# A scaled residual sum: the first 30.5 KiB of each partition taken from a contiguous head of the tensors

## The chip, the core and the metric

The kernel runs on one core of one Trainium2 chip. The core has a VectorE (DVE in the profile), a TensorE (PE), a ScalarE, a GpSimd (POOL) and a SyncE (SP), an on-chip memory of 128 partitions, and 16 DMA engines that move data between that memory and DRAM. In this kernel every transfer is issued from one queue, that of SyncE (SPq). The metric is the time of one execution on the device, in microseconds; the median of three runs is given.

## The reference

```python
B, S, D = 512, 32, 640          # x, fx: (B, S, D) bf16; alpha: (1,) bf16

def reference(x, fx, alpha):
    return x + alpha * fx
```

Each of x, fx and the output has 10,485,760 elements, 20.97 MB. The kernel reads 41.94 MB and writes 20.97 MB.

## The kernel before

Every tensor is seen as 128 rows, one for each partition, of 160 KiB each: partition p takes the elements from p x 81,920 on. The program counts in units of K = 512 elements, which are 1 KiB in bf16, so `x 0 64` is the load of the first 64 KiB of each partition's row, 128 rows of 64 KiB that lie 160 KiB apart in DRAM. (A row of over 64 KiB is cut into two equal pieces.)

There is one buffer `t` in the on-chip memory, of 207.5 KiB a partition (ROW = 160 and SPARE = 47.5). A piece of x from a to b is loaded to the places a to b of `t`, is added to in place, and is stored from there. The pieces of fx are put wherever there is space: the third number of an `f` step is its place in `t`. The places 95 to 160, for instance, first hold fx 0 to 65, and only later x 95 to 160; 160 to 207.5 first hold fx 65 to 112.5, and later fx 112.5 to 160. So the load of x from 95 on has to wait until the additions on 0 to 65 have read their fx, and the last two loads of fx wait for the additions on 65 to 95 and on 95 to 112.5.

The order is written out by hand in the string `PLAN`, one step a line, and the program issues the steps in that order, each on its engine:

- `f a b p` (L98 to L100): load fx from a to b to the place p; issued on SPq
- `x a b` (L95, L96): load x from a to b to its own place; SPq
- `a` (L102 to L110): load alpha eight times over, spread it over 128 partitions with a matmul, and copy the result to `a_f`
- `m a b` (L112, L113): multiply fx from a to b by alpha in place; VectorE, TENSOR_SCALAR
- `c a b` (L115, L116): add fx to x from a to b, in place of x; VectorE, TENSOR_TENSOR
- `s a b` (L118, L119): store from a to b; SPq
- `| m 112.5 134.5` behind a store: it also waits until that step has been done

An engine takes its steps strictly in order, and a step waits for the data it needs and for the space it overwrites. After the last store stands a no-operation on SPq (L131) that waits for everything but the last store. The function `of` (L86) says where in a DRAM tensor the piece from a to b of all partitions lies, and `xv`, `fv`, `ov` (L67) are the tensors as 128 rows.

The plan before, with its steps on one line each queue:

```text
SPq:     f 0 8 | a | f 8 65 | x 0 64 | x 64 95 | f 65 112.5 | x 95 160 |
         f 112.5 142.5 | f 142.5 160 | s 0 64 | s 64 128 | s 128 160
VectorE: m 0 8 | m 8 65 | c 0 8 | c 8 64 | c 64 65 | m 65 95 | c 65 95 |
         m 95 112.5 | c 95 112.5 | m 112.5 134.5 | m 134.5 142.5 |
         c 112.5 142.5 | m 142.5 160 | c 142.5 160
```

The first six loads wait for nothing. The first store waits for `m 112.5 134.5`, the second for `c 112.5 142.5`, the third for `c 142.5 160`.

Of the kernel before, what the change touches and what calls it, by code (L numbers as in the profile page):

```python
# [1 line left out]

# [4 lines left out]

ALU = mybir.AluOpType
F32 = mybir.dt.float32

P = 128
K = 512
ROW = 160
SPARE = 47.5

LANES = 8

PLAN = """
f 0 8 95
a
f 8 65 103  # L30
x 0 64
x 64 95
f 65 112.5 160
m 0 8
m 8 65
c 0 8
c 8 64
c 64 65
x 95 160
m 65 95  # L40
c 65 95
f 112.5 142.5 160
m 95 112.5
c 95 112.5
f 142.5 160 190
m 112.5 134.5
s 0 64 | m 112.5 134.5
m 134.5 142.5
c 112.5 142.5
m 142.5 160  # L50
c 142.5 160
s 64 128
s 128 160
"""


@with_exitstack
def kernel(
    ctx: ExitStack,
    tc: tile.TileContext,  # L60
    x: bass.AP,
    fx: bass.AP,
    alpha: bass.AP,
    out: bass.AP,
):
    nc = tc.nc
    xv, fv, ov = (  # L67
        t.flatten_outer_dims().rearrange("(p n) d -> p (n d)", p=P) for t in (x, fx, out)
    )
    assert xv.shape[1] == ROW * K  # L70

    consts = ctx.enter_context(tc.tile_pool(name="consts", bufs=1))
    psum = ctx.enter_context(tc.tile_pool(name="psum", bufs=1, space=bass.MemoryType.PSUM))
    flat = ctx.enter_context(tc.tile_pool(name="flat", bufs=1))
    ctx.enter_context(tc.manual_schedule())
    t = flat.tile([P, int((ROW + SPARE) * K)], x.dtype, name="t")
    info = mybir.DependencyInfo(mybir.DependencyClass.Sync, mybir.DependencyReason.DATA)

    lanes = {}
    lies = []  # L80
    done = []

    def at(a, b):
        return t[:, int(a * K) : int(b * K)]

    def of(v, a, b):  # L86
        return v[:, int(a * K) : int(b * K)]

    def place(a, b):
        for c, d, p in reversed(lies):  # L90
            if c <= a and b <= d:
                return at(p + a - c, p + b - c)
        raise ValueError(f"fx {a} to {b} lies nowhere in one piece")

    def load_x(a, b):  # L95
        done.append(nc.sync.dma_start(out=at(a, b), in_=of(xv, a, b)))  # L96

    def load_f(a, b, p):  # L98
        lies.append((a, b, p))
        done.append(nc.sync.dma_start(out=at(p, p + b - a), in_=of(fv, a, b)))  # L100

    def load_alpha():  # L102
        a_n = consts.tile([LANES, 1], alpha.dtype, name="a_n")
        done.append(nc.sync.dma_start(out=a_n[:], in_=alpha[None, :].to_broadcast([LANES, 1])))  # L104
        ones = consts.tile([1, P], alpha.dtype, name="ones")
        nc.vector.memset(ones[:], 1.0)  # L106
        a_ps = psum.tile([P, 1], F32, name="a_ps")
        done.append(nc.tensor.matmul(a_ps[:], ones[:], a_n[0:1, :], start=True, stop=True))  # L108
        lanes["a"] = consts.tile([P, 1], F32, name="a_f")
        nc.vector.tensor_copy(out=lanes["a"][:], in_=a_ps[:])  # L110

    def multiply(a, b):  # L112
        done.append(nc.vector.tensor_scalar_mul(place(a, b), place(a, b), lanes["a"][:]))  # L113

    def add(a, b):  # L115
        done.append(nc.vector.tensor_add(at(a, b), at(a, b), place(a, b)))  # L116

    def store(a, b):  # L118
        done.append(nc.sync.dma_start(out=of(ov, a, b), in_=at(a, b)))  # L119

    does = {"x": load_x, "f": load_f, "a": load_alpha, "m": multiply, "c": add, "s": store}
    begun = {}
    for step in filter(None, PLAN.split("\n")):
        step, *later = step.split(" | ")
        what, *numbers = step.split()
        does[what](*map(float, numbers))
        begun[step] = done[-1]
        for other in later:
            tc.add_manual_dep(done[-1].ins, begun[other].ins.name, info, reason="begins late")

    rest = nc.sync.nop(nofuse=True)  # L131
    for i in done[:-1]:
        tc.add_manual_dep(rest.ins, i.ins.name, info, reason="all but the last store")


# [1 line left out]
_INS = ['x', 'fx', 'alpha']  # L137
_OUTS = [((512, 32, 640), 'bfloat16')]


# [23 lines left out]
```

## Time and profile before

| | |
|---|---|
| median of 3 runs | 151.1 us (151.07 to 151.1) |
| the profiled execution | 151.11 us |
| its span, from the first to the last instruction | 149.3 us |
| DMA engines: busy share of the span | 98.0% |
| read from DRAM, written to it | 41.94 MB, 20.97 MB |
| mean rate over the span | 421 GB/s |
| VectorE busy | 66.5 us (45%) |
| of it additions (L116), multiplications (L113) | 43.6 us, 22.8 us |

The profiled execution's time, 151.11 us, is 1.8 us longer than its span: what lies before the first and after the last instruction is in the time and not in the span. The busy share of the DMA queue is the time that its packets took, over 16 engines and the span. A packet is one contiguous row or piece of a row, and every DMA adds some of a few bytes for its semaphore. In the slices of the page, and of the close-ups of the DMA, a packet is counted in the slice in which it starts, so long packets make high and low slices in turn while the engines are evenly busy.

Costliest groups by shape, with busy time and the mean of one, from the list of groups kept apart by shape:

| line | operation | elements a partition | count | mean ns |
|---|---|---|---|---|
| L116 | add | 28672 | 1 | 15086 |
| L116 | add | 15360 | 2 | 8157 |
| L116 | add | 8960 | 2 | 4826 |
| L116 | add | 4096 | 1 | 2293 |
| L113 | multiply | 29184 | 1 | 7820 |
| L113 | multiply | 15360 | 1 | 4220 |
| L113 | multiply | 11264 | 1 | 3152 |
| L113 | multiply | 8960 | 2 | 2546 |

### The profile page before, as it was taken

The page shows a single profiled execution, that of the slowest core. Times are in us where ns is not written, and L with a number is a line of the kernel's source. Part 1 is how long each engine was busy: PE and PEld are TensorE (multiplying, and loading weights), DVE is VectorE, ACT ScalarE, POOL GpSimd, SP SyncE. Part 2 cuts the span into 40 slices and gives each one's busy share as a digit, 9 for nine tenths or more (in the row PEclk, how much of TensorE's full clock was granted, in tenths as well). Part 3 has the DMA queues.
Part 4 walks back from the last instruction along what each step waited for, and adds up shares of the span by engine and source line. Part 5 has one row for each costly group of instructions (what it writes and reads, how often), then busy time and mean ns, then how long its engine had stood idle before and what let it go on. Part 6 is the DMA issues. An engine that isn't in the chain of part 4 may idle for free.

```text
span 149.3 us, 84 instructions
## 1 busy us (share of the span) xinstructions
PE 0.2 (0%) x1; PEld 0.1 (0%) x1; DVE 66.5 (45%) x16; POOL 0.2 (0%) x4
## 2 busy tenths in 40 slices
PE   0000000000000000000000000000000000000000
PEld 0000000000000000000000000000000000000000
DVE  0300008920069999029997093599997000000000
POOL 0000000000000000000000000000000000000000
DMA  5969998969699999999999999899896969697993
GB/s 147 603 281 500 500 461 351 562 281 562 281 408 451 438 417 443 456 429 428 428 428 428 417 444 469 378 526 492 351 562 281 562 281 562 281 562 307 456 474 167
DMA packets 1728, 62.92 MB, mean 421 GB/s; under 512 B 192, under 2 KB 192, under 8 KB 192
## 3 DMA queue, kind: packets, MB, share of 16 engines
q1 hardware_dynamic: 1728, 62.92, 98.0%
HBM read 41.94 MB, written 20.97 MB: 421 GB/s over the span
## 4 chain that ended last, share of the span: by engine, by line
DMA 38%; DVE 33%; another core or an unknown queue 4%; SPq 1%; issue 0%; DVEq 0%
DMA t<-in_x_dram 27%; DVE t L116 26%; DMA t<-in_fx_dram 11%; DVE t L113 7%; SPq L100 0%; SPq L104 0%; DVEq L116 0%
## 5 line engine op out<-in xcount | busy, mean ns | idle before, releaser
L116 DVE TENSOR_TENSOR t<-t 128x15360 bf16<-128x15360 bf16 (+4 forms) x7 | 43.6, 6252 | 16.6 <-DMA t<-in_x_dram 16.5
L113 DVE TENSOR_SCALAR t<-t,a_f 128x4096 bf16<-128x4096 bf16 (+4 forms) x7 | 22.8, 3265 | 25.7 <-DMA t<-in_fx_dram 25.7
L110 DVE COPY a_f<-a_ps 128x1 f32<-128x1 f32 x1 | 0.2, 159 | 5.2 <-PE a_ps L108 5.2
L106 DVE MEMSET ones<- 1x128 bf16 x1 | 0.2, 165 | 0.8 <-PEq L148 0.8
L108 PE MATMUL a_ps<-a_n,ones 1*128 1x1 bf16 x1 | 0.2, 158 | 6.0 <-DMA a_n<-in_alpha_dram 6.0
L148 POOL MEMSET const-bfloat16-1.0<- 128x1 bf16 x1 | 0.1, 102 | 0.0
L148 POOL MEMSET const-uint8-127<- 128x1 uint8 x1 | 0.1, 102 | 0.0
L148 POOL MEMSET const-float32-1.0<- 128x1 f32 x1 | 0.1, 99 | 0.0
L108 PEld LDWEIGHTS <-ones 1*128 1x128 bf16 x1 | 0.1, 98 | 1.0 <-DVE ones L106 1.0
L148 POOL MEMSET const-float32-0.0<- 128x1 f32 x1 | 0.1, 98 | 0.2 <-issue 0.2
## 6 DMA issues: line engine op xcount, KB each, us to landing
t<-in_x_dram SPq DMA_DIRECT2D x1, 8320.0 KB, 25.8
t<-in_fx_dram SPq DMA_DIRECT2D x1, 7296.0 KB, 21.4
t<-in_fx_dram SPq DMA_DIRECT2D x1, 6080.0 KB, 63.0
out_dram<-t SPq DMA_DIRECT2D x1, 4096.0 KB, 33.7
t<-in_x_dram SPq DMA_DIRECT2D x1, 3968.0 KB, 49.3
t<-in_fx_dram SPq DMA_DIRECT2D x1, 3840.0 KB, 16.4
t<-in_fx_dram SPq DMA_DIRECT2D x1, 2240.0 KB, 9.5
t<-in_fx_dram SPq DMA_DIRECT2D x1, 1024.0 KB, 5.0
```

The source lines that it names most:

```text
L106: nc.vector.memset(ones[:], 1.0)
L108: done.append(nc.tensor.matmul(a_ps[:], ones[:], a_n[0:1, :], start=True, stop=True))
L110: nc.vector.tensor_copy(out=lanes["a"][:], in_=a_ps[:])
L113: done.append(nc.vector.tensor_scalar_mul(place(a, b), place(a, b), lanes["a"][:]))
L116: done.append(nc.vector.tensor_add(at(a, b), at(a, b), place(a, b)))
L148: nc = _bacc.Bacc("TRN2", target_bir_lowering=False, num_devices=1)
```

## The change

Each tensor is divided in DRAM into a head and a tail. The head is its first 128 x 30.5 KiB, one contiguous stretch, and partition p takes the p-th 30.5 KiB of it; the tail is the rest, and partition p takes the p-th 129.5 KiB of that. A partition's places 0 to 30.5 are the head's, 30.5 to 160 the tail's. Since x, fx and the output are divided in the same way, the sum is the same, element by element. Rows of the head lie 30.5 KiB apart, rows of the tail 129.5 KiB, and no transfer may cross 30.5.

The plan is cut accordingly. The load of fx 8 to 65 becomes two (8 to 30.5, 30.5 to 65), so that there are nine loads of x and fx instead of eight. The first two loads of x are 30.5 to 94.5 (64 KiB) and then 0 to 30.5, which is all of the head in one piece; the additions that follow take 30.5 to 65 first and 0 to 8 and 8 to 30.5 after it. The border at 95 moves to 94.5, the one at 142.5 to 142. The stores are 0 to 30.5, 30.5 to 94.5 and 94.5 to 160, instead of 64, 64 and 32 KiB.

```diff
+HEAD = 30.5
 PLAN = """
 f 0 8 95
 a
-f 8 65 103
-x 0 64
-x 64 95
+f 8 30.5 103
+f 30.5 65 125.5
+x 30.5 94.5
+x 0 30.5
 f 65 112.5 160
 m 0 8
-m 8 65
+m 8 30.5
+m 30.5 65
+c 30.5 65
 c 0 8
-c 8 64
-c 64 65
-x 95 160
-m 65 95
-c 65 95
-f 112.5 142.5 160
-m 95 112.5
-c 95 112.5
-f 142.5 160 190
+c 8 30.5
+x 94.5 160
+m 65 94.5
+c 65 94.5
+f 112.5 142 160
+m 94.5 112.5
+c 94.5 112.5
+f 142 160 189.5
 m 112.5 134.5
-s 0 64 | m 112.5 134.5
-m 134.5 142.5
-c 112.5 142.5
-m 142.5 160
-c 142.5 160
-s 64 128
-s 128 160
+s 0 30.5 | m 112.5 134.5
+m 134.5 142
+c 112.5 142
+m 142 160
+c 142 160
+s 30.5 94.5
+s 94.5 160
 """
...
-    xv, fv, ov = (
-        t.flatten_outer_dims().rearrange("(p n) d -> p (n d)", p=P) for t in (x, fx, out)
-    )
-    assert xv.shape[1] == ROW * K
+    xv, fv, ov = (t.flatten_outer_dims().rearrange("n d -> (n d)") for t in (x, fx, out))
+    assert xv.shape[0] == P * ROW * K
...
     def of(v, a, b):
-        return v[:, int(a * K) : int(b * K)]
+        assert b <= HEAD or a >= HEAD
+        at_head = b <= HEAD
+        part = v[: int(P * HEAD * K)] if at_head else v[int(P * HEAD * K) :]
+        shift = 0 if at_head else HEAD
+        return part.rearrange("(p n) -> p n", p=P)[:, int((a - shift) * K) : int((b - shift) * K)]
```

## The prediction

> **What bounds the kernel now.** I read the page's DMA lines first, then the waits of the compute engine and of the issuing queue, then the timeline, and last two close-ups of the DMA at the start and the end.
>
> The page, parts 2 and 3:
>
> ```profile
> span 149.3 us, 84 instructions
> ...
> DMA packets 1728, 62.92 MB, mean 421 GB/s; under 512 B 192, under 2 KB 192, under 8 KB 192
> ...
> q1 hardware_dynamic: 1728, 62.92, 98.0%
> ```
>
> All 62.92 MB go through one queue whose 16 engines are busy 98.0% of the span; 2.0% of 149.3 us, 3.0 us, is all that is idle. VectorE is busy for 66.5 us, 45%. So the DMA engines set the time, and three things can change it: time per byte, number of pieces, and moments in which the queue has nothing to do. The waits, VectorE's and then the issuing queue's:
>
> ```profile
> DVE t L113 <- DMA t<-in_fx_dram: 25.7, 3, 15.3
> DVE t L116 <- DMA t<-in_x_dram: 16.5, 2, 11.6
> ```
>
> ```profile
> SPq L96 <- DVE t L116: 56.5, 1, 56.5
> SPq L100 <- DVE t L116: 24.2, 2, 12.4
> ```
>
> VectorE waits for loads, while the queue's late issues (the load of x from 95, the last two of fx) wait for VectorE, because the buffer space they write has to be read first. Such a wait costs nothing as long as the engines still have older transfers. The timeline (start, duration, in brackets the idle time before) shows by how much they have:
>
> ```profile
> 3.09 0.51 SPq L100 DMA_DIRECT2D t<-in_fx_dram  x1
> ...
> 22.99 7.82 DVE L113 TENSOR_SCALAR t<-t,a_f 128x29184 bf16<-128x29184 bf16 x1 [15.34 <-DMA t<-in_fx_dram]
> 42.41 17.63 DVE L116 TENSOR_TENSOR t<-t 128x4096 bf16<-128x4096 bf16 x3 [11.61 <-DMA t<-in_x_dram]
> 60.07 0.38 SPq L96 DMA_DIRECT2D t<-in_x_dram  x1
> 66.14 4.22 DVE L113 TENSOR_SCALAR t<-t,a_f 128x15360 bf16<-128x15360 bf16 x1 [6.10 <-DMA t<-in_fx_dram]
> 70.40 8.16 DVE L116 TENSOR_TENSOR t<-t 128x15360 bf16<-128x15360 bf16 x1
> 78.47 2.55 DVE L113 TENSOR_SCALAR t<-t,a_f 128x8960 bf16<-128x8960 bf16 x1
> 78.58 12.53 SPq L100 DMA_DIRECT2D t<-in_fx_dram  x2
> 85.94 4.83 DVE L116 TENSOR_TENSOR t<-t 128x8960 bf16<-128x8960 bf16 x1 [4.91 <-DMA t<-in_x_dram]
> 94.97 4.35 DVE L113 TENSOR_SCALAR t<-t,a_f 128x11264 bf16<-128x11264 bf16 x2 [4.21 <-DMA t<-in_fx_dram]
> 98.15 17.05 SPq L119 DMA_DIRECT2D out_dram<-t  x3
> ```
>
> Where VectorE waited for a load, its start marks the landing. From 22.99 to 42.41 the 64 KiB rows of x came: 19.42 us, 0.3034 us per KiB of each partition. From 42.41 to 66.14 came 31 + 47.5 KiB: 0.3023. From 66.14 to 85.94 the 65 KiB rows: 19.80 us, 0.3046. From 85.94 to 94.97 30 KiB: 0.3010. From 94.97 to the last landing at 148.6 (the issuing queue's last wait) 17.5 + 160 KiB: 0.3022. Loads and stores, long rows and short ones, move at one rate, and no stretch has a hole. What is left is the start and the end. Close-ups of the DMA, 40 slices each of 1.5 to 5.5 us and of 146 to 148.6 us (a packet counts where it starts):
>
> ```profile
> DMA  0099940010299399398399599399399799999999
> ```
>
> ```profile
> DMA  0000000999999990000000000000000000000000
> ```
>
> The first packets start at about 1.7 us and the next only from 2.4 us on, although an 8 KiB row takes 0.309 us in the trace's DMA records later in this same load: the first 14 packets last 0.69 to 1.44 us there, and those 128 rows cost each engine 0.69 us more than 8 x 0.309 us. At the end the engines start their last packets between 146.5 and 147.0 us, some 0.5 us apart.
>
> **Part 1, more pieces.** 1728 packets are 192 small ones (16 for each of 12 DMAs) and 1536 = 12 sets of 128 rows; the eleven large DMAs make twelve sets because the 65 KiB row is cut in two. After the change there are ten load sets (the load of fx 8 to 65 becomes two, and 65.5 KiB is again cut in two) and four store sets (30.5, 64, and 65.5 in two): 14 sets, 1792 packets, and 13 x 16 = 208 small ones. Bytes stay. The price of a set isn't a row of its own. The 65 KiB load in two sets against the 64 KiB load in one gives 19.80 - 19.42 - 0.30 = +0.08 us; the 30 KiB load against the 64 KiB one gives the other bound, 9.03 - 30 x 0.3034 = -0.07 us, nothing or below, since landings are read only to a packet or so. The DMA records lie between: 65,536 bytes take 2.418 us and 8,192 bytes 0.309, which leaves 7 or 8 ns a packet, and 8 packets an engine and set make 0.06 us. I take 0.05 to 0.06: two sets cost 0.11 us, bounds -0.14 to +0.16. The sixteen additional small packets, one an engine at 9 ns in the same records, are 0.01 us. This lies on the path, since the engines have no idle time to hide it.
>
> **Part 2, the order of the work.** Each late issue has to come before the older transfers run out, by at least the time from issue to first packet (0.73 to about 1.75 us for the first load: 1.0 us). VectorE's durations for the new sizes come from the rows: additions are 15.086 us for 28672 elements and 8.157 for 15360, so 0.5205 ns an element and 0.16 us fixed; multiplications 7.82 us for 29184 and 4.22 for 15360, so 0.2604 ns an element.
> - Load of x from 94.5. The first 129 KiB of loads are the same in sum, so x 30.5 to 94.5 lands at 42.41 + 0.06 = 42.5. The three additions after it have the same 33,280 elements as the three now: 9.36 us for 30.5 to 65, ending at 51.8; x 0 to 30.5 lands at 42.5 + 30.5 x 0.3023 = 51.7, just in time; then 2.29 and 6.16 us, to 60.3. Issue at 60.3 instead of 60.07, with older transfers until 66.2: 5.9 us ahead, 4.9 after the 1.0. If x 0 to 30.5 is some tenths late, the additions and this issue are late by as much, inside these 4.9 us.
> - fx 112.5 to 142: multiplication 4.15 and addition 8.02 from 66.2 end at 78.4. x from 94.5 (0.5 KiB more) lands at 86.1: 7.7 us ahead.
> - fx 142 to 160: the addition on 94.5 to 112.5 starts at 86.1 and takes 4.96, so 91.1; fx 112.5 to 142 runs until 86.1 + 29.5 x 0.301 = 95.0: 3.9 us ahead, 2.9 after the 1.0.
> - First store: it waits for the multiplication on 112.5 to 134.5, 3.15 us from 95.0, so 98.2; loads run until 95.0 + 18 x 0.302 = 100.4. 2.2 us ahead, 1.2 after the 1.0. This is the tightest, and not tighter than now (98.15, with 17.5 KiB from 94.97, until 100.3).
> - The first store is now only 30.5 KiB, over at 109.6; the second waits for nothing that is still to come (its addition ended long before) and is issued right behind it at 98.6. The third waits for VectorE's last addition, at about 115, and is due at 100.4 + 94.5 x 0.3022 = 129.0.
> - The issuing queue gets one DMA more at the start, 0.35 us (L100's median); its six first large loads are then out at about 4.0 us instead of 3.6, and every one of them but the first is out long before its turn.
> So the order costs 0: what hides it is the older transfer each time. Without that cover, every us late would be a us of the end. The last packets are 32.75 KiB instead of 32, at most 0.03 us more for an engine.
>
> **Part 3, the addresses.** The 128 rows of a load lie 160 KiB apart now; then 30.5 KiB apart in the head and 129.5 in the tail. The trace of before has the 160 KiB pitch alone, so the price is bounded by its rows: the slowest stretch (0.3046 us per KiB) against the mean after the start (0.3022 to 0.3034), 0.8% at most, and the fastest (0.3010), 0.4%. Over 0.81 of the 146 us of transfers (the tail), that is -0.5 to +0.9 us. I take 0, because loads and stores of all sizes and offsets stand within these few tenths of a per cent, which looks like a limit of the engines and not of the addresses. For the start, the bounds are all of the lost 0.69 us and a second one lost; I take 0 there too, the nearest row being this very load.
>
> The Trainium skill, page "DMA: Bandwidth & Descriptors", section "Latency and other measured facts", speaks against pitches that are large powers of two (207 GB/s at 512 KiB a partition, 103 at 4 MiB, where 214 is full; 4 KiB more restored it, 192 bytes more did not); 160 KiB at a full, even rate agrees with it, and 129.5 is 1.5 KiB past 128 KiB. By its 3.3% at 512 KiB the tail would take 3.9 us longer, an estimate, and no row here shows it.
>
> **Sum.** The profiled execution took 151.11 us, 1.8 us around the span of 149.3, and the median is 151.1, so the two agree. 151.1 + 0.11 (sets) + 0.01 (small packets) + 0 (order) + 0 (addresses) = 151.2 us. Its own range is 150.9 to 151.4: -0.14 to +0.16 for the sets, and a tenth more for start and end.
>
> **The rivals.**
> 1. The start gets better. All rows now begin 160 KiB apart, on multiples of 32 KiB, and each of the 16 engines loses 0.69 us; the head's 30.5 KiB pitch puts them on different ones. For: the loss is in the first load alone, and it is the load whose pitch changes most. Against: a first packet also has a delay that no layout removes; even the shortest of the first 14 exceeds its later duration by 0.38 us. So 0.69 - 0.38 = 0.3 us may go, and if the engines start closer together some of the 0.5 us between them at the end, 0.1 to 0.2 on average. 151.2 - 0.45 = 150.75, down to 150.4.
> 2. The tail's pitch makes packets slower. For: it is near a power of two, and 0.81 of the bytes use it. Against: 160 KiB, 5 x 32, shows no such loss although every row begins on the same multiple. At the slow bound, +0.9 us: 152.1. It decides from 0.2% on each tail packet (0.2 us of 118, with the 0.12 of the sets). It would show in x 30.5 to 94.5, at over 19.5 us, and in the stores.
> 3. The queue runs dry before the first store, the place with the least cover. It needs a delay of over 1.2 us, for instance from a slower start of the store; 0.3 us beyond that gives 151.5, one us 152.2. Against: the store is issued as far ahead as now.
> That the change does nothing is part of the forecast: data, sums and rate stay, only addresses and cuts differ.
>
> **How the numbers follow.** Forecast 0.45, rival 1 0.32, rival 2 0.16, rival 3 0.07. A measurement of this kernel tells about 0.2%, 0.3 us, from no change, so the forecast is "within", rival 1 faster, 2 and 3 slower: 0.32, 0.45, 0.23. The range of 150.4 to 151.9 holds the forecast, nearly all of rival 1 and the nearer half of 2 and 3; some 0.15 lies outside, most of it above.
>
> **What would show it.** 2000 packets, 208 under 512 B, and a queue share of about 98%. VectorE's first large addition at 42.5, issue of x at about 60.3, the multiplication on 112.5 to 134.5 at 95.0, the first store at 98.2. For rival 1: the close-up of the start without the gap between 2.1 and 2.4 us, and every later landing earlier by the same amount. For rival 2: stretches of the tail over 0.305 us per KiB, those of the head not. For rival 3: an idle DMA near 100 us. The prediction is wrong if the rate per KiB moves by over 0.2%, or the start by over 0.3 us.

## The result, and the profile after

| | before | after |
|---|---|---|
| median of 22 runs each | 151.1 us (150.9 to 151.31) | 151.33 us (151.0 to 151.77) |
| ratio to before, 95% interval | | 1.0018 [1.0012, 1.0024] |
| profiled execution, its span | 151.11, 149.3 us | 151.54, 149.8 us |

The changed kernel takes 0.18% longer, 0.27 us (the medians differ by 0.23), and its times spread more: from lowest to highest 0.77 us, where the kernel before has 0.41. The profiled execution is one of the longer ones, so its trace shows the loss rather large.

The page after, parts 2 and 3:

```profile
span 149.8 us, 86 instructions
...
DMA packets 2000, 62.92 MB, mean 420 GB/s; under 512 B 208, under 2 KB 208, under 8 KB 208
...
q1 hardware_dynamic: 2000, 62.92, 97.8%
```

The count is as forecast, 2000 packets with 208 small ones, and the engines are still nearly always busy. The timeline after:

```profile
...
22.96 4.82 DVE L120 TENSOR_SCALAR t<-t,a_f 128x17664 bf16<-128x17664 bf16 x1 [7.25 <-DMA t<-in_fx_dram]
42.38 17.63 DVE L123 TENSOR_TENSOR t<-t 128x17664 bf16<-128x17664 bf16 x3 [14.61 <-DMA t<-in_x_dram]
60.04 0.38 SPq L103 DMA_DIRECT2D t<-in_x_dram  x1
65.95 4.15 DVE L120 TENSOR_SCALAR t<-t,a_f 128x15104 bf16<-128x15104 bf16 x1 [5.94 <-DMA t<-in_fx_dram]
...
78.19 13.02 SPq L107 DMA_DIRECT2D t<-in_fx_dram  x2
85.90 4.96 DVE L123 TENSOR_TENSOR t<-t 128x9216 bf16<-128x9216 bf16 x1 [5.21 <-DMA t<-in_x_dram]
94.79 4.28 DVE L120 TENSOR_SCALAR t<-t,a_f 128x11264 bf16<-128x11264 bf16 x2 [3.93 <-DMA t<-in_fx_dram]
97.97 17.10 SPq L126 DMA_DIRECT2D out_dram<-t  x3
```

Read as before, the landings give the rate of each stretch: 42.38 - 22.96 = 19.42 us for 64 KiB of each partition, 0.3034 us per KiB (0.3034 before); 23.57 for 78 KiB, 0.3022 (0.3023); 19.95 for 65.5 KiB, 0.3046 (0.3046); 8.89 for 29.5 KiB, 0.3014 (0.3010). Up to 94.79 us nothing is lost. The rest, 18 KiB of loads and 160 of stores, lasts until the last landing at 149.03 (the issuing queue's last wait): 54.24 us, 0.3047 where it was 0.3022. All of the loss stands behind 94.79 us. The close-up of 146 to 148.6 us shows its form (a packet counts where it starts; 40 slices of 0.065 us):

```profile
DMA  0090000999999900000009000000000000000000
```

Fifteen engines start their last packet by 146.9 us, as before, and a single one starts it at about 147.4. The kernel ends with that engine. The DMA records have the start, the duration and the bytes of every packet, but name no engine; the packets of one engine are told by each starting where the one before it ended. Followed back in this way, the late engine lost its time at 94.31 us, in its first row of the last load of fx: that packet lasted 0.54 us longer than the later rows of the same load. The start is as it was, in the close-up of 1.5 to 5.5 us:

```profile
DMA  0099951804018969959959977973955959999900
```

The 128 rows of the first load cost each engine 0.68 us more than 8 times 0.309 us; before it was 0.69.

### The profile page after: what moved, and what is told of

Read it like the earlier page. It is cut to its first block, busy times and chain, and to the rows that moved or that the text cites. A ratio compares the mean times of both kernels' runs of the same rounds, so it can differ in the third digit from the quotient of the medians.

```text
span 149.8 us, 86 instructions
## 1 busy us (share of the span) xinstructions
PE 0.2 (0%) x1; PEld 0.1 (0%) x1; DVE 66.7 (45%) x17; POOL 0.2 (0%) x4
## 4 chain that ended last, share of the span: by engine, by line
DMA 38%; DVE 33%; another core or an unknown queue 4%; SPq 1%; issue 0%; DVEq 0%
DMA t<-in_x_dram 27%; DVE t L123 26%; DMA t<-in_fx_dram 11%; DVE t L120 7%; SPq L107 1%; SPq L111 0%; DVEq L123 0%
## 5 line engine op out<-in xcount | busy, mean ns | idle before, releaser
L123 DVE TENSOR_TENSOR t<-t 128x15104 bf16<-128x15104 bf16 (+4 forms) x7 | 43.6, 6251 | 19.9 <-DMA t<-in_x_dram 19.8
L120 DVE TENSOR_SCALAR t<-t,a_f 128x9216 bf16<-128x9216 bf16 (+6 forms) x8 | 23.0, 2884 | 22.2 <-DMA t<-in_fx_dram 22.2
```

## The experiments

Twelve kernels, in three groups; each was timed beside the kernel before on the same chip. All compute the reference in full.

### 1. The new plan with the old addresses

`of` gives rows 160 KiB apart again; the plan is the new one. (The lines with head and tail that go are left out here.)

```diff
     def of(v, a, b):
-        ...
+        return v.rearrange("(p n) -> p n", p=P)[:, int(a * K) : int(b * K)]
```

> The plan of the changed kernel, every step and size of it, with the old addresses (rows 160 KiB apart). If the pieces alone make the kernel longer (two sets more, 0.12 us, as forecast), it stands where the changed kernel stands, ratio to before 1.001 to 1.002, with 2000 packets and a first load whose rows take as long. If the addresses do it, head or tail, the ratio goes back to 1.000 to 1.0008.

Measured 151.48 us, ratio 1.0031 [1.0018, 1.0044]. The head is gone and the loss is still there, so it is in the plan. It is even larger than the 1.001 to 1.002 expected, which two sets of 0.06 us can't make. Its trace shows the same form at the end, with two late engines instead of one (146 to 148.6 us):

```profile
DMA  0900900099990099000090090000000000000000
```

In its DMA records one engine's first row of the last load of fx lasts 0.99 us longer than the later ones, another's 0.31 us.

### 2 and 3. The load cut, and the stores cut, each alone in the kernel before

```diff
-f 8 65 103
+f 8 30.5 103
+f 30.5 65 125.5
```

(`m` and `c` cut at 30.5 as well.)

> The kernel before with only the load of fx 8 to 65 made two (8 to 30.5, 30.5 to 65): one set of 128 rows and one DMA more. By the price per set +0.06 us, ratio 1.0004; if what the changed kernel lost hangs on the loads' cuts, 1.001 or more.

```diff
-s 0 64 | m 112.5 134.5
-s 64 128
-s 128 160
+s 0 30.5 | m 112.5 134.5
+s 30.5 94.5
+s 94.5 160
```

> The kernel before with only the stores changed to 30.5, 64 and 65.5 KiB: one set more, in the last store. By the price per set +0.06 us, ratio 1.0004. If the loss is in the stores (the last one long and in two pieces, the engines ending further apart), ratio 1.0015 or more, and the last packets of the trace spread as in the changed kernel, over 0.9 us instead of 0.5.

Measured 1.0008 [0.9999, 1.0016] and 1.0000 [0.9991, 1.0008]. Neither alone makes the loss, and each is consistent with +0.06 us for one more set. The spread of the times stays narrow: 151.04 to 151.3 and 150.94 to 151.17.

### 4. A tail pitch of exactly 128 KiB

```diff
-HEAD = 30.5
+HEAD = 32
```

All cuts at 30.5 move to 32, and the borders at 94.5 and 142 go back to 95 and 142.5; the first load of x is 32 to 95, and the stores are 32, 63 and 65 KiB.

> The changed kernel with the head at 32 KiB, so that the tail's rows lie exactly 128 KiB apart, and the pieces cut at 32 and 95 accordingly: the same count of sets. If pitches near a power of two cost anything, this one costs most: 3.3% of 118 us, +3.9 us by the page's 512 KiB figure, and at least +0.9 us by the slow bound of the rows. If the engines alone set the rate, it equals the changed kernel, ratio to before 1.001 to 1.002.

Measured 151.09 us, 1.0005 [0.9997, 1.0014]. A pitch of a whole power of two costs nothing that can be seen here, far from 3.9 us: what the Trainium skill's page "DMA: Bandwidth & Descriptors" tells of pitches from 512 KiB up (section "Latency and other measured facts") doesn't reach down to rows of 32 KiB and more at 128 KiB. What I had not expected is that this kernel is better than the changed one, with the same number of sets. Beside the head's size and the cuts that follow it, it differs in one thing: the border is at 95. So I looked at what the border decides.

### The theory: the lead of the last load of fx

The last load of fx overwrites the places of fx 95 to 112.5 (94.5 to 112.5), so it is issued when the addition on them ends, and that addition waits for all of x from the border on. The engines come to this load when fx 112.5 to 142.5 (142) is over. Half a KiB less at the border makes that earlier load 0.15 us shorter and that addition 0.13 us longer. In the changed kernel the addition runs from 85.90 to 90.86 and the load is issued at 90.89; in the kernel before from 85.94 to 90.77, and at 90.79. The two issues, before and then after:

```profile
90.79 0.33 SPq L100 DMA_DIRECT2D t<-in_fx_dram  x1
```

```profile
90.89 0.33 SPq L107 DMA_DIRECT2D t<-in_fx_dram  x1
```

The time from the issue of a load to the first packet of the first engine that comes to it is called its lead here. The DMA records show rows that last longer than the later rows of the same load, at 93.8 to 94.5 us, on a few engines. Behind the first load, these two kernels have rows that stand out by more than 0.06 us in this load alone. The kernel before has two of them as well (0.49 and 0.31 us); the prediction's rate for that stretch, 0.3022, averages over them.

### 5 and 6. The border alone, by half a KiB and by two

The kernel before with 95 and 142.5 moved to 94.5 and 142, and to 93 and 140.5; addresses, stores and the count of sets as they were. For 93 (the multiplications and the other additions, whose ends move likewise, are left out here):

```diff
-x 64 95
+x 64 93
...
-x 95 160
+x 93 160
...
-f 112.5 142.5 160
+f 112.5 140.5 160
...
-c 95 112.5
+c 93 112.5
-f 142.5 160 190
+f 140.5 160 188
```

> The kernel before, old addresses, one load of fx 8 to 65, its own stores, with only the border at 95 moved to 94.5 and the one at 142.5 to 142. Theory lead: the last load of fx is issued only some 3 us before the first engines come to it, which is not enough for all of them (their first packets there last 0.3 to 1.0 us longer than later ones); moving the border takes about 0.28 us of that lead (0.15 for the shorter load before it, 0.13 for the longer addition). Then this alone gives a ratio of 1.001 to 1.002, a wider spread of times, and long first packets of that load. Theory pieces: the loss is in the number of sets and DMAs, which don't change here: 1.000 and no such packets beyond those of the kernel before.

> The same with the border at 93 (and 140.5): by theory lead 1.1 us of the lead go (4 times as much as at 94.5), more engines are held and for longer, ratio 1.004 or more, up to the whole 1.1 us (1.007). By theory pieces 1.000.

Measured 151.47 us, 1.0024 [1.0015, 1.0033], spread 150.94 to 151.75, and 152.77 us, 1.0114 [1.0101, 1.0126]. Half a KiB of border does alone what the whole change does; 1.0024 is somewhat more than the 1.001 to 1.002 expected. (The one profiled execution at 94.5 took 150.96 us and shows the long rows without a late end.) At 93 the loss is 1.7 us, more than the 1.1 us of lead that go. The timeline there, and the close-up of 146 to 150 us (slices of 0.1 us):

```profile
85.92 5.36 DVE L116 TENSOR_TENSOR t<-t 128x9984 bf16<-128x9984 bf16 x1 [6.06 <-DMA t<-in_x_dram]
91.31 0.33 SPq L100 DMA_DIRECT2D t<-in_fx_dram  x1
94.36 4.08 DVE L113 TENSOR_SCALAR t<-t,a_f 128x11264 bf16<-128x11264 bf16 x2 [3.08 <-DMA t<-in_fx_dram]
97.54 0.35 SPq L119 DMA_DIRECT2D out_dram<-t  x1
```

```profile
DMA  9009799909709000770700007000770000000000
```

The issue is at 91.31, and the first engine is there at 93.26 by the records, 1.95 us later. The engines now start their last packets over 2.3 us instead of 0.5: ten end at most 0.3 us behind the last of the kernel before, and six by 0.7 to 2.0 us.

### 7 and 8. The lead given back, before and after

The last part of x is loaded in two, so that the addition doesn't wait for all of it. (65 KiB were cut in two already; the count of sets stays.)

```diff
-x 95 160
+x 95 112.5
+x 112.5 160
```

> The kernel before with the load of x 95 to 160 as two loads, 95 to 112.5 and 112.5 to 160 (two sets, as its 65 KiB in two pieces are now, and one DMA more). The addition on 95 to 112.5 then doesn't wait for all of x, and the last load of fx is issued at about 86 instead of 90.8, a lead of 8 us. By theory lead no long packet in that load, and a ratio of 0.998 to 1.000 with a narrower spread. By theory pieces 1.000 to 1.0004.

> The changed kernel with its load of x 94.5 to 160 as two, 94.5 to 112.5 and 112.5 to 160. By theory lead the long packets at 94 us and the late engine at the end are gone, and what stays is the price of the sets: ratio to before 1.0000 to 1.0008. By theory pieces it stays at 1.0018.

Measured 151.05 us, 1.0000 [0.9991, 1.0009] for the kernel before with it, and 151.13 us, 1.0005 [0.9996, 1.0014] for the changed kernel with it, with a spread of 151.06 to 151.25. The two last loads of fx in the changed kernel with the split, and its close-up of 146 to 148.6 us:

```profile
78.20 7.85 SPq L108 DMA_DIRECT2D t<-in_fx_dram  x2
```

```profile
DMA  0000000999999990000000000000000000000000
```

The second issue ends at 78.20 + 7.85 = 86.05 instead of 91.2, and no engine is late. In its records no row after the first load lasts 0.04 us longer than its like. What is left of its loss, 0.0005, is the size of the price of the sets and can't be told from nothing.

### 9 and 10. Two checks of it

The border at 93 with x 93 to 160 as two loads (93 to 112.5, 112.5 to 160); and experiment 1 with the same split of its x.

> The border at 93, which took 1.0114 of the kernel before, with the load of x 93 to 160 as two, 93 to 112.5 and 112.5 to 160. By theory lead all of the loss goes, 0.999 to 1.001, because the last load of fx is issued some 8 us ahead again. If the border itself costs (sizes of rows, length of the additions, the first store's time), most of the 1.0114 stays.

> The plan of the changed kernel with the old addresses, as in the first experiment, and its load of x 94.5 to 160 as two. With the lead given back only pieces and addresses are left. If the addresses cost and gain nothing it equals the changed kernel with the same split (1.0005, 0.9996 to 1.0014); a head that helped the start would leave this one slower by 0.002 to 0.003; a tail pitch that costs would leave it faster by 0.001 or more.

Measured 150.94 us, 0.9992 [0.9969, 1.0015], and 151.08 us, 0.9998 [0.9977, 1.0020]; the kernel before had a median of 150.94 us in this group, and one of its runs took 152.91, which widens the intervals. The border's whole 1.1% is gone with the sizes at the border as they were, so it was the lead and not the sizes of rows. Old and new addresses with the lead given back are equal as far as these runs tell. A gain of 0.3 us from the head (0.002) would have left experiment 10 above experiment 8 by as much; it stands 0.0007 below it, with intervals that together leave room for about 0.002 either way.

### 11 and 12. The first store's place

The store is held back until `m 112.5 134.5`. Here it isn't:

```diff
-s 0 64 | m 112.5 134.5
+s 0 64
```

once in the kernel of experiment 7, and once in that of experiment 6.

> The kernel before with x 95 to 160 split (1.0000) and with the first store no longer held back until the multiplication on 112.5 to 134.5: it is issued at about 86.3, 12 us earlier, still behind all loads in the queue. If a short lead costs stores as it costs loads (the engines come to the first store some 1.3 us after it is issued), it gets faster, 0.998 to 0.9995, and the long packets of the first store's rows go; if a store needs no lead, 1.000; if the store's presence in the queue hinders the loads, slower, 1.001 or more.

> The border at 93 without the split, and the first store not held back: it is issued right behind the last load of fx, at about 91.8. With the border at 93 the late engines stood twice, in their first packet of that load (94 us) and in its sixth (98.2 to 98.4 us, 0.7 us after the store was issued). If the second stand comes from the store's issue, it goes here or moves with the issue, and the ratio falls from 1.0114 to 1.006 or less; if both come from the load's own lead, 1.011 stays.

Measured 151.73 us, 1.0039 [1.0017, 1.0060] for the first: a store that is in the queue early makes it slower. Busy time in the stretch from 96 to 98 us, the last two numbers being the DMA's share and GB/s; first experiment 7, then experiment 11:

```profile
96.00:98.00 2.00, 0.00 (x0) 0.00 (x0) 2.00 (x2) 0.00 (x0) 1.00 1.01 430
```

```profile
96.00:98.00 2.00, 0.00 (x0) 0.00 (x0) 2.00 (x2) 0.00 (x0) 1.00 1.03 385
```

The engines are as busy from 96 to 98 us, and start less: 385 instead of 430 GB/s. In the records sixteen rows at 98.0 to 98.5 us last 0.47 to 0.66 us longer than their like, and ten at 97.2 to 97.5 us 0.1 to 0.5 us longer; they are the last but one and the one before it of the eight that each engine loads before it comes to the store. The engines end at 148.48 us on average, at 147.90 in experiment 7.

For the second, 1.0109 [1.0059, 1.0158], from five runs of 152.26 to 153.91 us (a sixth took 155.07 and isn't in the ratio); 1.006 or less was expected if the second stand, in experiment 6's sixth rows at 98.2 to 98.3 us, came from the store's issue. That stand did shrink (0.5 us at most at 97 to 98.3 us, 0.7 to 0.9 before), but the first grew, to up to 1.7 us on eight engines at 93.2 to 93.6, with the store issued 0.4 us after the load. The sum is the same, and the two can't be told apart by it.

### The lead and the long rows, side by side

One profiled execution each, from the timelines and the DMA records: when the last load of fx is issued, when the first engine comes to it, the time between, the same time as a mean over the first packets of all 16 engines, and by how much the first rows that stand out at 93.5 to 94.5 us exceed their like.

| kernel | issue | first engine | lead | mean of 16 | longer by, us | ratio |
|---|---|---|---|---|---|---|
| 6, border 93 | 91.31 | 93.26 | 1.95 | 2.3 | 0.56, 0.45, 0.38, 0.37 | 1.0114 |
| 1, new plan, old rows | 91.02 | 93.91 | 2.89 | 3.05 | 0.99, 0.31 | 1.0031 |
| after | 90.89 | 93.89 | 3.00 | 3.19 | 0.54, 0.14, 0.10 | 1.0018 |
| 5, border 94.5 | 90.73 | 93.81 | 3.08 | 3.27 | 0.46, 0.33 | 1.0024 |
| before | 90.79 | 93.90 | 3.11 | 3.41 | 0.49, 0.31 | |
| 3, stores | 90.77 | 93.88 | 3.11 | 3.44 | 0.35 | 1.0000 |
| 4, head 32 | 90.68 | 93.91 | 3.24 | 3.50 | none | 1.0005 |
| 2, load cut | 90.84 | 94.14 | 3.30 | 3.48 | none | 1.0008 |
| 7, 8, 9, 10 (split) | 85 to 86 | 93 to 94 | 8 | 8 | none | 1.0000, 1.0005, 0.9992, 0.9998 |

The first engine's lead hardly tells the kernel before (3.11) from the border at 94.5 (3.08), which lost 0.24%. The mean over the engines does, though it was chosen after the traces were seen and rests on one of each kernel: the four kernels that lost time have 2.3 to 3.27 us, and those that lost none that can be told 3.41 us and more. It is no threshold for one engine: the rows held in the kernels before, after, 1, 3 and 5 began 2.95 to 3.42 us after the issue, and in each of these kernels other engines that began within the same times weren't held.

The kernel before stands at the edge. Its own long rows fell on engines that were early enough not to be last: they were over at 95.06 and 95.14 us, and the first row of the engine that came last at 95.17. In the changed kernel the longest of them was over at 95.53, some 0.6 us behind all the others. That with a little less lead an engine that ends the kernel is held more often, and that the times spread for this reason, fits; one profiled execution each can't show how often.

## Why the prediction was right, and where a step of it failed

The forecast was 151.2 us, within 0.2% of before, and 151.33 was measured, 1.0018. The frame held: the DMA engines set the time, the rate per KiB is the same to 0.0004 us in each stretch up to 94.79 us, and order and issues came out within 0.3 us of the times worked out (the load of x from 94.5 at 60.04 for 60.3, the load of fx 112.5 to 142 at 78.19 for 78.4, the last load of fx at 90.89 for 91.1, the first store at 97.97 for 98.2). In the last stretch the prediction's own sign of being wrong, a rate per KiB that moves by over 0.2%, did come: 0.3047 for 0.3022, 0.8%. The cause is one engine of 16 that ends late, and not the rate; the sign couldn't tell the two apart.

The sets: two more at 0.055 us each, 0.12 us with the small packets. The changed kernel with its lead given back has 1.0005, 0.08 us, with an interval that goes from nothing to about 0.2 us. The size fits; that it is above nothing isn't shown.

The addresses: taken as 0, and they are 0 as far as can be told. The start costs what it did, 0.68 us for 0.69, so rival 1 is out (over the traces of all these kernels it is 0.47 to 0.72 us, and both of these ends have the old addresses); pitches of 129.5 and 128 KiB run at the rate of 160 KiB, so rival 2 is out.

The step that failed is "so the order costs 0", in the bullet on fx 142 to 160: "3.9 us ahead, 2.9 after the 1.0". The change does take from this lead, and the lead was not ample. The wait that this bullet worked out is the one that decides: the runs give it 1.0018 - 1.0005 = 0.0013 of before, about 0.2 us (the intervals are [1.0012, 1.0024] and [0.9996, 1.0014]; half a KiB of border alone gave 1.0024 [1.0015, 1.0033]). Two things were wrong in it. First, 3.9 us is the time until the whole earlier load has landed, on the last engine; the first engine comes to the next load 0.9 us before that, at 93.89, and 3.0 us is what it has. Secondly, 1.0 us is the time from an issue to the first packet of the first engine. In that same first load the records have the last engine's first packet at 2.62 us and the longest of the first packets over at 3.19, 1.9 and 2.46 us after the issue at 0.73. But even the late end wouldn't have given the need: rows were held that began up to 3.42 us after their issue. An idle queue's first load was no measure of what a load needs in a busy one, and what sets that need stays open.

Rival 3 had the mechanism, a queue that isn't fed in time, but put it before the first store as "the place with the least cover", at 1.2 us. The store has still less lead and isn't held; it is the load before it that is. So the forecast's number came out of a sum with one term missing, and was near because the missing term is small. In that step this was luck: 0.18% stands just inside the 0.2%, and its interval reaches past it. By the same test the border at 93 would have passed too, with 94.36 - 91.31 = 3.05 us ahead and 2.05 after the 1.0, and that kernel lost 1.7 us.

## What to carry to other kernels

Where DMA engines are busy all the time, look at how long before its turn each late transfer is issued, and count to when the engines come to it, not to the landing of the transfer before. Here a load wants to be issued some 3.4 us or more ahead as a mean over the engines, so a border that frees its space half a KiB sooner or later can outweigh the pieces and addresses that a change is about; cutting the load in front, so that the addition which frees the space needn't wait for all of it, gave 8 us of lead for one more DMA and no additional set. And when times spread more after a change, ask which engine ends last, and where that one lost its time.

None of the twelve beat the kernel before: the border at 93 with the split (0.9992 [0.9969, 1.0015]) and the split alone (1.0000) equal it.

## What the runs showed of the hardware that had not been expected

- A load issued 8 us before the first engine came to it, or 3.2 to 3.3 us, showed no long first row; with 2.9 to 3.1 us one to three of the 16 engines had a first row that lasted 0.1 to 1.0 us longer; with 1.95 us there were four of 0.37 to 0.56 us, and the kernel lost 1.7 us. Which engines are held changes from trace to trace, and the order in which they come doesn't tell it: in the kernel before the first to come is held, in the changed kernel the last is held longest. What in the engine or in front of it takes that time stays open.
- The first store showed no such need: where it was held back, the first engine came to it 1.1 to 1.9 us after its issue, and its rows lasted at most 0.05 us longer. On the contrary, a store issued 12 us ahead, behind loads that were still running, made late rows of these loads 0.5 us longer and the kernel 0.4% [0.17, 0.60]. Holding it back was worth that much in the kernel with the split. Why is not shown.
- With the border at 93 the three engines that end last stood a second time, for 0.75 to 0.93 us in their sixth of eight rows, which began at 98.2 to 98.3 us, some 0.7 us after the store was issued. That is more than the 0.37 to 0.45 us of their first rows, so the larger part of the loss came then. It fits with the point above, but the run that was to separate them left it open.
